# First half's scores ahead of the second half's transposes, the k loads in one run, tile 0's v on SyncE's queue, ScalarE's tables first

## The chip, the cores and the metric

The kernel runs on one core of one Trainium2 chip. A core has five engines that work beside each other: TensorE (PE, matrix products), VectorE (DVE), ScalarE (ACT), GpSimd (POOL) and SyncE (SP, which here only issues transfers). Each engine works through its own list of instructions in order. Transfers between the chip's main memory (HBM) and the on-chip memory are issued by an engine and carried out by 16 DMA engines that all queues share. In this kernel GpSimd's transfers show up in the profile as queue q0 ("software_dynamic"), SyncE's as q1 ("hardware_dynamic"), ScalarE's one transfer as q10.

The metric is the device time of one execution in microseconds. Three runs of the kernel before took 316.43, 315.59 and 316.18 us: a median of 316.18.

## The reference

Retention (attention with a decay in place of the softmax) over 8 batches, 8 heads, 576 positions, 64 numbers per head, followed by a two-layer network with a gated nonlinearity:

```
B, H, S, D_ = 8, 8, 576, 64
scores = (1/sqrt(D_)) * q @ k.T
gamma  = 1 - 2 ** (-5 - head)
Dmat   = where(i >= j, gamma ** (i - j), 0)
x      = (scores * Dmat) @ v            # -> [B * S, H * D_] = [4608, 512]
h      = x @ w_in                       # [4608, 2048]
g      = h * tanh(log(1 + exp(h)))
out    = g @ w_out                      # [4608, 512]
```

Inputs and output are float32; the kernel multiplies in bfloat16.

## The kernel before

The 4,608 rows of x are cut into 36 chunks of 128 rows, and four chunks make a tile of 512 rows. The first two tiles are special: they hold the first chunk (positions 0 to 127) of each of the 8 batches, where nothing comes from earlier positions, so that x is only masked scores times v. Tile 0 is batches 0 to 3. This text is about how tile 0 gets started; from tile 1 on the kernel is unchanged.

For tile 0 the work goes in these steps, each in two halves of two batches (g = 0 is batches 0 and 1, g = 1 is batches 2 and 3):

1. Loads. q of batch b (256 KB, float32) is issued by SyncE, line 120. k of batch b is issued by GpSimd and turned into bfloat16 on the way (`load_first_qk`, line 106). v comes in pairs of batches, 512 KB each, from GpSimd (`load_first_v`, line 117). The first layer's weights w_in come in four loads of 512 columns (512 KB each in bfloat16, from twice as many bytes in HBM), also from GpSimd (`load_w_in`, line 86). q and k are read in runs of 2 KB (eight positions of one head), v in runs of 256 B (one position of one head).
2. q is cast to bfloat16 by one instruction per batch, on different engines (lines 442, 448, 145).
3. `f_transpose(0, g, i, parts)` turns k (i = 1) or q (i = 0) of two batches on TensorE, 32 small products into PSUM, and copies the result out in two parts, on ScalarE or VectorE (line 202).
4. `f_scores(0, g)` makes 16 products (line 211) and VectorE multiplies each batch by the decay mask (line 215, one instruction per batch, `sm`).
5. `f_v(0, b, engine)` casts v of a batch (line 222). `f_out(0, b, engine)` multiplies masked scores by v (line 236) and copies into x transposed (line 239).
6. `g1(0, f, half)` is the first layer for 128 of the 2,048 columns. For f = 0 to 3 it is done on the first two batches' rows (`half[0]`, line 466) and later on the others (`half[1]`, line 470). From f = 4 on all 512 rows go together (line 497). ScalarE applies the nonlinearity (Mish, line 373).

`keep_warm(n)` issues n products of zeros on TensorE, to keep it busy in stretches where it would wait. ScalarE loads a table before its first exponential and another before its first Mish; a one-number Mish (`warm`, line 457) brings the second load on early. The decay mask is made from `dist` by 8 VectorE instructions (line 153) and one exponential (line 440); `gq` and `gv`, used from tile 1 on and in `f_state`, are exponentials of `ex` (lines 447, 455, 456), which comes from `pos`.

The order of all this is written out by hand: each engine does its instructions in the order of the program, and waits only on data and on buffers. So the order in which GpSimd meets its loads, its casts (`pool` in the calls) and its small set-up instructions is the order of the source, from line 121 on and then from line 440 on. Behind GpSimd's casts of v in the source stand the loads of tile 1's k and q (line 472), the second layer's weights w_out (line 474) and further loads.

q, k and v of tile 0 lie in two buffers that later hold the results of the first layer: `stage` (k, q in bfloat16 and v) and `gts[0]` (q in float32).

Of the kernel before, what the change touches and what calls it, by code (L numbers as in the profile page):

```python
# [10 lines left out]
F32 = mybir.dt.float32  # L11
BF16 = mybir.dt.bfloat16
# [5 lines left out]
def kernel(  # L18
# [18 lines left out]
    nc = tc.nc  # L37
    B, H, S, D = q.shape
    assert (B, H, S, D) == (8, 8, 576, 64)
    P = 128  # L40
# [21 lines left out]
    consts = ctx.enter_context(tc.tile_pool(name="consts", bufs=1))  # L62
    wpool = ctx.enter_context(tc.tile_pool(name="weights", bufs=1))
    first = ctx.enter_context(tc.tile_pool(name="first", bufs=1))
# [7 lines left out]
    ps_sc = ctx.enter_context(tc.tile_pool(name="ps_sc", bufs=2, space=PS))  # L72
    ps_st = ctx.enter_context(tc.tile_pool(name="ps_st", bufs=1, space=PS))
    ps_h = ctx.enter_context(tc.tile_pool(name="ps_h", bufs=2, space=PS))
    ps_o = ctx.enter_context(tc.tile_pool(name="ps_o", bufs=1, space=PS))
# [9 lines left out]
    def load_w_in(f0, n):  # L85
        nc.gpsimd.dma_start(out=w_in_t[:, :, ds(f0, n)], in_=w_in_r[:, :, ds(f0, n)])
# [8 lines left out]
    stage = gp.tile([P, nF, NCH * P], BF16, name="gT")  # L95
    gts = {0: gp.tile([P, nF, NCH * P], BF16, name="gT")}
    q0 = gts[0][:, H:nF, :].bitcast(F32).rearrange("p (b a) c -> p b (a c)", a=2)
    v0 = {}
    fst = {}

    def load_first_qk(t, i, b):

        name = ("qb", "kb")[i]
        if t not in fst:
            fst[t] = {"qb": stage[:, 0:4, :], "kb": stage[:, 4:8, :], "vb": {}}
        nc.gpsimd.dma_start(out=fst[t][name][:, b, :],  # L106
                            in_=(q, k)[i][4 * t + b, :, 0:P, :].rearrange("h (g r) d -> g h (r d)", r=8))

    def load_first_v(b):

        if b < 4:
            pair = stage[:, ds(8 + 2 * b, 4), :].bitcast(F32).rearrange("p a (c d) -> p (a c) d", d=D)
        else:
            pair = first.tile([P, 2 * H, D], F32, name="vpair", bufs=2)
        for e in range(2):
            v0[b + e] = pair[:, ds(H * e, H), :]
        nc.gpsimd.dma_start(out=pair, in_=v[ds(b, 2), :, 0:P, :].rearrange("b h p d -> p (b h) d"))

    for b in range(4):
        nc.sync.dma_start(out=q0[:, b, :], in_=q[b, :, 0:P, :].rearrange("h (g r) d -> g h (r d)", r=8))  # L120
    for b in range(2):
        load_first_qk(0, 1, b)

    zeros = consts.tile([P, 512], BF16)
    nc.vector.memset(zeros, 0.0)
# [4 lines left out]
                   allow_small_or_imprecise_dtypes=True)  # L130
    nc.gpsimd.affine_select(out=dist, in_=dist, compare_op=OP.is_ge, fill=1.0e6,
                            base=0, pattern=[[1, P]], channel_multiplier=-1)
    ident = consts.tile([P, P], BF16)
    make_identity(nc, ident)
    for b in (2, 3):
        load_first_qk(0, 1, b)
    pos = consts.tile([P, 5], F32)
    nc.gpsimd.iota(pos, pattern=[[P, 5]], base=0, channel_multiplier=1,
                   allow_small_or_imprecise_dtypes=True)
    nc.gpsimd.iota(pos[64:P, 4:5], pattern=[[1, 1]], base=512, channel_multiplier=1,  # L140
                   allow_small_or_imprecise_dtypes=True)
    load_first_v(0)
    load_w_in(0, 512)
    load_first_v(2)
    nc.gpsimd.tensor_copy(fst[0]["qb"][:, 3, :], q0[:, 3, :])
    for i in range(1, 4):
        load_w_in(512 * i, 512)
    mask = consts.tile([P, P], F32)
    mask2 = consts.tile([P, P], F32)
    lg = [math.log(1.0 - 2.0 ** (-5.0 - h)) for h in range(H)]  # L150
# [13 lines left out]
    def keep_warm(n, pool=ps_o, name="ops"):  # L164
        idle = pool.tile([P, 512], F32, name=name)
        for _ in range(n):
            nc.tensor.matmul(idle, lhsT=zeros[:, 0:P], rhs=zeros, start=True, stop=True)
# [14 lines left out]
    def f_transpose(t, g, i, parts):  # L182

        name = ("qb", "kb")[i]
        out_t = first.tile([P, H, P], BF16, name=name + "T", bufs=2)
        n = 8 // len(parts)
        moves = []
        for j, (pool, tname, copy) in enumerate(parts):
            tp = pool.tile([P, 2, 8, P] if tname == "sc" else [P, 8, P], BF16, name=tname)
            tp = (tp[:, 0] if tname == "sc" else tp)[:, 0:n]  # L190
            for r in range(n):
                if t == 1:
                    mix = fst[1][name, "mix", g][:, n * j + r]
                    nc.tensor.transpose(tp[:, r, :], mix.rearrange("p x d -> p (x d)"), ident)
                else:
                    for x in range(2):
                        nc.tensor.transpose(tp[ds(64 * x, 64), r, :],
                                            fst[0][name][:, 2 * g + x, ts(n * j + r, D)], ident)
            moves.append((copy, out_t.rearrange("p h (g r) -> p h g r", r=8)[:, :, :, ds(n * j, n)],
                          tp.rearrange("p r (g h) -> p h g r", h=H)))  # L200
        for copy, to, src in moves:
            copy(to, src)
        fst[t][name, g] = out_t

    def f_scores(t, g, between=None):
        qT, kT = fst[t]["qb", g], fst[t]["kb", g]
        scs = [ps_sc.tile([P, 2, NP, P], F32, name="sc").rearrange("p a b i -> p (a b) i") for _ in range(2)]
        for h in range(H):
            for x in range(2):
                r = ds(64 * x, 64)  # L210
                nc.tensor.matmul(scs[x][:, h, :], lhsT=kT[r, h, :], rhs=qT[r, h, :], start=True, stop=True)  # L211
        for x in range(2):
            b = 2 * g + x
            sm = first.tile([P, H, P], BF16, name="sm0", bufs=4)
            nc.vector.tensor_tensor(sm, scs[x], dmask, op=OP.mult)  # L215
            fst[t]["sm", b] = sm
            if between and x == 0:
                between()

    def f_v(t, b, copy):  # L220
        vb = first.tile([P, H, D], BF16, name="vb", bufs=4)
        copy(vb, v0[4 * t + b])
        fst[t]["vb"][b] = vb

    def f_out(t, b, copy):
        if b == 0:
            xts[t] = xp.tile([P, KC, NCH * P], BF16, name="xT")
        vb = fst[t]["vb"][b]
        if t == 0:
            pool, name = ((ps_h, "hp"), (ps_h, "hp"), (ps_st, "st"), (ps_o, "ops"))[b]  # L230
            ot = pool.tile([P, NP, P], F32, name=name)
        else:
            ot = ps_sc.tile([P, 2, NP, P], F32, name="sc")[:, 0]
        for p in range(NP):
            for e in range(2):
                nc.tensor.matmul(ot[ds(64 * e, 64), p, :], lhsT=vb[:, 2 * p + e, :],
                                 rhs=fst[t]["sm", b][:, 2 * p + e, :],
                                 start=(p == 0), stop=True, skip_group_check=True)
        copy(xts[t][:, :, ts(b, P)], ot)  # L239
# [196 lines left out]
    dve, act, pool = nc.vector.tensor_copy, nc.scalar.copy, nc.gpsimd.tensor_copy  # L436
# [1 line left out]

    half = (slice(0, 2 * P), slice(2 * P, 4 * P))
    nc.scalar.activation(dmask, dmask, AX.Exp, bias=lnd[:, 0:1])  # L440
    for b in range(2):
        dve(fst[0]["qb"][:, b, :], q0[:, b, :])
    keep_warm(8)
    f_transpose(0, 0, 1, [(ps_h, "hp", act), (ps_h, "hp", dve)])
    f_transpose(0, 0, 0, [(ps_st, "st", act), (ps_o, "ops", dve)])
    for h in range(H):
        nc.vector.tensor_scalar(ex[:, :, h], pos, lg[h], None, op0=OP.mult)
    act(fst[0]["qb"][:, 2, :], q0[:, 2, :])
    f_transpose(0, 1, 1, [(ps_h, "hp", act), (ps_h, "hp", act)])
    keep_warm(2, ps_sc, "sc")  # L450
    f_scores(0, 0)
    keep_warm(3, ps_st, "st")
    f_transpose(0, 1, 0, [(ps_st, "st", act), (ps_o, "ops", act)])
    keep_warm(4, ps_h, "hp")
    nc.scalar.activation(gq, ex, AX.Exp)
    nc.scalar.activation(gv, ex, AX.Exp, scale=-1.0)
    nc.scalar.activation(warm, lnd, AX.Mish)
    f_v(0, 0, pool)
    f_v(0, 1, pool)
    f_scores(0, 1, lambda: f_out(0, 0, dve))  # L460
    f_out(0, 1, act)
    f_v(0, 2, pool)
    f_v(0, 3, act)
    keep_warm(3, ps_st, "st")
    for f in range(4):
        g1(0, f, half[0])
    f_out(0, 2, act)
# [14 lines left out]
    for b in (4, 6):  # L482
        load_first_v(b)
# [147 lines left out]
```

## Time and profile before

| what | value |
|---|---|
| time of three runs | 316.43, 315.59, 316.18 us, median 316.18 |
| the profiled execution | 317.75 us, of which the span from first to last instruction is 316.0 |
| TensorE (PE) busy | 302.7 us, 96% of the span |
| VectorE, ScalarE, GpSimd busy | 135.3, 111.7, 143.0 us |
| TensorE's mean granted clock | 0.989 of full speed |
| moved by the DMA engines | 42.85 MB, 136 GB/s on average |
| q0 (GpSimd), q1 (SyncE) | 27.27 MB in 48,640 packets; 15.08 MB in 24,832 packets |

How to read the rows. In a timeline a row gives the start, the time taken, the engine, the line of the program (L197 is line 197), the operation, output <- inputs, the shape and how many such instructions are merged; in square brackets stands how long the engine had been idle before, and what ended the wait. A row of stages gives the stretch, its length, busy time and count for each engine, the clock that TensorE was granted, the share of time in which the DMA engines were busy (it can be above 1, since packets overlap) and GB/s. A row of a queue gives packets, megabytes and the packets' time as a share of 16 engines. All times are microseconds from the start of the span. In the tables of the trace `gT` stands for the two buffers in which q, k and v of tile 0 are put.

### The profile page before, as it was taken

The numbers are of one execution on the slowest core, as the hardware profiler recorded it, in microseconds if no ns is written. First come the engines' busy times: TensorE is split into PE (matmuls) and PEld (weight loads), VectorE is DVE, ScalarE is ACT, GpSimd is POOL, SyncE is SP. The second block draws the span as 40 slices with busy tenths as digits, with TensorE's granted clock in tenths as the row PEclk, the third lists the DMA queues.
The fourth block names the chain that finished last, engine by engine and source line by source line (L and its number), as shares of the span: only waits on it lengthen the run. The fifth ranks groups of instructions, "written<-read, shape, count | busy, mean of one in ns | idle before, by whom it ended". The sixth has DMA issues, their size and how long they took to land.

```text
span 316.0 us, 5807 instructions
## 1 busy us (share of the span) xinstructions
PE 302.7 (96%) x2428; PEld 153.4 (49%) x2468; DVE 135.3 (43%) x198; ACT 111.7 (35%) x185; POOL 143.0 (45%) x178
## 2 busy tenths in 40 slices
PE   5779999999999999998999999999999999999995
PEld 2454554555555554544545454545454545444444
DVE  3553148487636535353535453535354332001111
ACT  3476525753353533332232333332323232333300
POOL 8587849889684976356373536252010000000000
PEclk9599999999999999999999999999999999999999
DMA  7999999999992899999999999991514000010031
GB/s 176 232 207 204 221 207 197 274 163 183 234 183 79 139 163 164 187 83 210 153 181 88 214 136 180 122 168 36 98 37 100 35 33 35 34 33 33 35 97 69
DMA packets 73642, 42.85 MB, mean 136 GB/s; under 512 B 58640, under 2 KB 64528, under 8 KB 73616
## 3 DMA queue, kind: packets, MB, share of 16 engines
q0 software_dynamic: 48640, 27.27, 64.0%
q1 hardware_dynamic: 24832, 15.08, 25.9%
q8 instruction: 19, 0.31, 0.5%
q10 hardware_dynamic: 144, 0.13, 0.1%
q14 instruction: 7, 0.06, 0.1%
HBM read 38.80 MB, written 9.44 MB: 153 GB/s over the span
## 4 chain that ended last, share of the span: by engine, by line
PE 74%; DMA 20%; POOL 3%; issue 1%; ACT 0%; DVE 0%; POOLq 0%
PE hp L371 31%; PE ops L386 26%; DMA qkT<-qks 9%; PE hp L386 4%; DMA w_out_t<-in_moe_w_out_dram 4%; DMA qraw<-in_q_dram 4%; PE sc L301 2%; DMA vraw<-in_v_dram 2%; PE st L333 2%; DMA gT<-in_k_dram 2%; PE sc L353 1%; PE sc L358 1%; PE sc L288 1%; PE hp L414 1%; POOL gT L106 1%
## 5 line engine op out<-in xcount | busy, mean ns | idle before, releaser
L371 PE MATMUL hp<-xT,w_in_t 128*128 128x512 bf16 (+1 forms) x562 | 141.4, 373 | 2.9 <-DVE xT L239 0.8
L373 ACT ACTIVATE gT<-hp 128x512 bf16<-128x512 f32 (+1 forms) x148 | 86.8, 586 | 157.7 <-PE hp L371 143.9
L386 PE MATMUL ops<-w_out_t,gT 128*128 128x512 bf16 x430 | 110.1, 379 | 0.4
L371 PEld LDWEIGHTS <-w_in_t 128*128 128x128 bf16 x592 | 55.1, 98 | 62.8 <-issue 2.1
L386 PEld LDWEIGHTS <-gT 128*128 128x128 bf16 x496 | 48.3, 98 | 58.0 <-issue 0.8
L422 DVE COPY res<-ops 128x512 f32<-128x512 f32 x28 | 19.3, 688 | 83.4 <-PE ops L386 79.6
L336 DVE TENSOR_TENSOR ssb<-st,diag 128x512 bf16<-128x512 f32 x32 | 21.9, 685 | 49.6 <-PE st L333 49.6
L263 POOL DMA_DIRECT2D qraw<-in_q_dram x24 | 22.1, 921 | 40.5 <-DVE qks L273 38.0
L279 POOL TENSOR_TENSOR vs<-vraw,gv 128x512 bf16<-128x512 f32 x28 | 29.9, 1077 | 20.2 <-issue 14.0
L305 DVE TENSOR_TENSOR sm<-sc,mask 128x1024 bf16<-128x1024 f32 x28 | 33.1, 1216 | 5.9 <-PE sc L301 5.9
L263 POOL DMA_DIRECT2D vraw<-in_v_dram x24 | 21.7, 903 | 2.6 <-DMA vpair<-in_v_dram 1.5
L263 POOL DMA_DIRECT2D qks<-in_k_dram x24 | 21.6, 899 | 1.2 <-DMA w_out_t<-in_moe_w_out_dram 0.9
L273 DVE TENSOR_TENSOR qks<-qraw,gq 128x512 bf16<-128x512 f32 x28 | 19.9, 746 | 0.0
L362 DVE CAST xT<-sc 128x512 bf16<-128x512 f32 x24 | 15.3, 680 | 0.0
L386 PE MATMUL hp<-w_out_t,gT 128*128 128x512 bf16 x61 | 14.7, 379 | 0.2
L215 DVE TENSOR_TENSOR sm<-sc,dmask 128x1024 bf16<-128x1024 f32 x8 | 9.5, 1220 | 8.4 <-PE sc L211 8.4
L289 ACT COPY qkT<-sc 128x1024 bf16<-128x1024 bf16 x10 | 10.1, 1010 | 8.0 <-PE sc L288 8.0
L267 POOL DMA_DIRECT2D qraw<-in_q_dram x8 | 5.6, 708 | 14.1 <-DVE qks L273 14.1
L301 PE MATMUL sc<-qkT 64*128 64x128 bf16 x224 | 9.4, 218 | 1.5 <-DMA qkT<-qks 1.5
L301 PEld LDWEIGHTS <-qkT 64*128 64x128 bf16 x224 | 6.3, 94 | 6.7 <-issue 3.4
L353 PE MATMUL sc<-qkT,ssb 128*64 128x128 bf16 (+1 forms) x224 | 9.5, 213 | 0.0
L358 PE MATMUL sc<-sm,vs 128*64 128x128 bf16 x192 | 9.4, 219 | 0.0
(102 smaller groups left out, 193.3 us busy)
## 6 DMA issues: line engine op xcount, KB each, us to landing
out_dram<-res SPq DMA_DIRECT2D x31, 256.0 KB, 3.9
qraw<-in_q_dram POOLq DMA_DIRECT2D x24, 256.0 KB, 5.5
vraw<-in_v_dram POOLq DMA_DIRECT2D x24, 256.0 KB, 8.3
qks<-in_k_dram POOLq DMA_DIRECT2D x24, 128.0 KB, 7.3
w_in_t<-in_moe_w_in_dram POOLq DMA_DIRECT2D x4, 512.0 KB, 10.6
w_out_t<-in_moe_w_out_dram POOLq DMA_DIRECT2D x4, 512.0 KB, 10.4
gT<-in_q_dram SPq DMA_DIRECT2D x4, 256.0 KB, 4.9
gT<-in_k_dram POOLq DMA_DIRECT2D x8, 128.0 KB, 6.9
```

What stands on the lines that cost most here:

```text
L263: nc.gpsimd.dma_start(out=t, in_=src[b, :, ds(P * c, P), :].rearrange("h p d -> p h d"))
L273: nc.vector.tensor_tensor(live[n]["qks"][:, 0], live[n]["q"], gq[:, c, :].unsqueeze(2).to_broadcast([P, H, D]), op=OP.mult)
L279: nc.gpsimd.tensor_tensor(vs, live[n]["v"], gv[:, c, :].unsqueeze(2).to_broadcast([P, H, D]), op=OP.mult)
L301: nc.tensor.matmul(sc[:, e, p, :], lhsT=qk[r, 1, p, :], rhs=qk[r, 0, p, :], start=True, stop=True)
L305: nc.vector.tensor_tensor(sm.rearrange("p e n i -> p (e n) i"), sc.rearrange("p e n i -> p (e n) i"), m.unsqueeze(1).to_broadcast([P, 2 * ...
L336: nc.vector.tensor_tensor(ssb.rearrange("p e n d -> p e (n d)"), st.rearrange("p n d -> p (n d)").unsqueeze(1).to_broadcast([P, 2, NP * 64 ...
L353: nc.tensor.matmul(ot[ds(64 * e, 64), p, ds(i0, iw)], lhsT=st_sb[bb, cc][:, e, p, :], rhs=qk[:, 0, p, ds(i0, iw)], start=(i0 == 0 and p == ...
L362: nc.vector.tensor_copy(xts[t][:, :, ts(s, P)], ot)
L371: nc.tensor.matmul(hp[:, cols], lhsT=w_in_t[:, c, ts(f, P)], rhs=xts[t][:, c, cols], start=(c == 0), stop=(c == KC - 1))
L373: nc.scalar.activation(gts[t][:, f, cols], hp[:, cols], AX.Mish)
L386: nc.tensor.matmul(ops, lhsT=gts[t][:, f, ts(s, P)], rhs=w_out_t[:, f, :], start=(f == 0), stop=(f == nF - 1))
L422: copy(ot, ops)
```

## The change

In the loads:

- tile 0's v goes from two loads of two batches on GpSimd to four loads of one batch on SyncE, behind the four loads of q;
- the four k loads stand together on GpSimd, behind the two instructions that make `dist`, and ahead of `pos` and the identity; before, two stood at the very start and two after the identity;
- three of the four w_in loads then follow at once, ahead of the cast of batch 3's q; the fourth follows the cast.

In the order written out by hand:

- `ex`, `gq`, `gv` and the first Mish, with its table load, move ahead of the transposes;
- `f_scores(0, 0)` moves ahead of the second half's transposes of k; the second half's transposes of q follow directly on those of k;
- the cast of batch 2's q goes from ScalarE to VectorE, the cast of batch 3's v from ScalarE to GpSimd, so that all four v casts stand together on GpSimd;
- `f_out(0, 0)` and `f_out(0, 1)` stand ahead of `f_scores(0, 1)`; before, `f_out(0, 0)` stood between its two masks and `f_out(0, 1)` after it;
- the numbers of warming products are 9, 2, 3 and 4 in place of 8, 2, 3, 4 and 3.

```
     def load_first_v(b):
-        if b < 4:
-            pair = stage[:, ds(8 + 2 * b, 4), :].bitcast(F32).rearrange("p a (c d) -> p (a c) d", d=D)
-        else:
-            pair = first.tile([P, 2 * H, D], F32, name="vpair", bufs=2)
+        pair = first.tile([P, 2 * H, D], F32, name="vpair", bufs=2)
...
     for b in range(4):
         nc.sync.dma_start(out=q0[:, b, :], in_=q[b, :, 0:P, :].rearrange("h (g r) d -> g h (r d)", r=8))
-    for b in range(2):
-        load_first_qk(0, 1, b)
+    for b in range(4):
+        v0[b] = stage[:, ds(8 + 2 * b, 2), :].bitcast(F32).rearrange("p a (c d) -> p (a c) d", d=D)
+        nc.sync.dma_start(out=v0[b], in_=v[b, :, 0:P, :].rearrange("h p d -> p h d"))
...
     nc.gpsimd.affine_select(out=dist, in_=dist, compare_op=OP.is_ge, fill=1.0e6,
                             base=0, pattern=[[1, P]], channel_multiplier=-1)
-    ident = consts.tile([P, P], BF16)
-    make_identity(nc, ident)
-    for b in (2, 3):
+    for b in range(4):
         load_first_qk(0, 1, b)
     pos = consts.tile([P, 5], F32)
...
-    load_first_v(0)
-    load_w_in(0, 512)
-    load_first_v(2)
+    ident = consts.tile([P, P], BF16)
+    make_identity(nc, ident)
+    for i in range(3):
+        load_w_in(512 * i, 512)
+
     nc.gpsimd.tensor_copy(fst[0]["qb"][:, 3, :], q0[:, 3, :])
-    for i in range(1, 4):
-        load_w_in(512 * i, 512)
+    load_w_in(1536, 512)
...
     nc.scalar.activation(dmask, dmask, AX.Exp, bias=lnd[:, 0:1])
-    for b in range(2):
-        dve(fst[0]["qb"][:, b, :], q0[:, b, :])
-    keep_warm(8)
-    f_transpose(0, 0, 1, [(ps_h, "hp", act), (ps_h, "hp", dve)])
-    f_transpose(0, 0, 0, [(ps_st, "st", act), (ps_o, "ops", dve)])
     for h in range(H):
         nc.vector.tensor_scalar(ex[:, :, h], pos, lg[h], None, op0=OP.mult)
-    act(fst[0]["qb"][:, 2, :], q0[:, 2, :])
-    f_transpose(0, 1, 1, [(ps_h, "hp", act), (ps_h, "hp", act)])
-    keep_warm(2, ps_sc, "sc")
-    f_scores(0, 0)
-    keep_warm(3, ps_st, "st")
-    f_transpose(0, 1, 0, [(ps_st, "st", act), (ps_o, "ops", act)])
-    keep_warm(4, ps_h, "hp")
     nc.scalar.activation(gq, ex, AX.Exp)
     nc.scalar.activation(gv, ex, AX.Exp, scale=-1.0)
     nc.scalar.activation(warm, lnd, AX.Mish)
-    f_v(0, 0, pool)
-    f_v(0, 1, pool)
-    f_scores(0, 1, lambda: f_out(0, 0, dve))
+    for b in range(2):
+        dve(fst[0]["qb"][:, b, :], q0[:, b, :])
+    keep_warm(9)
+    f_transpose(0, 0, 1, [(ps_h, "hp", act), (ps_h, "hp", dve)])
+    f_transpose(0, 0, 0, [(ps_st, "st", act), (ps_o, "ops", dve)])
+    dve(fst[0]["qb"][:, 2, :], q0[:, 2, :])
+    keep_warm(2, ps_sc, "sc")
+    f_scores(0, 0)
+    f_transpose(0, 1, 1, [(ps_h, "hp", act), (ps_h, "hp", act)])
+    f_transpose(0, 1, 0, [(ps_st, "st", act), (ps_o, "ops", act)])
+    for b in range(4):
+        f_v(0, b, pool)
+    keep_warm(3, ps_h, "hp")
+    f_out(0, 0, dve)
     f_out(0, 1, act)
-    f_v(0, 2, pool)
-    f_v(0, 3, act)
-    keep_warm(3, ps_st, "st")
+    f_scores(0, 1)
+    keep_warm(4, ps_st, "st")
     for f in range(4):
         g1(0, f, half[0])
     f_out(0, 2, act)
```

## The prediction

> **What bounds the kernel now.** I read the page's head, then busy time by stages, then TensorE's timeline of the first 24 us, the waits there, and last the packets of each DMA queue in short windows. The stages come first, since an average over the whole says nothing about a change in the first 22 us:
>
> ```profile
> span 316.0 us, 5807 instructions
> ...
> 8.55:12.00 3.45, 2.16 (x22) 1.28 (x25) 1.54 (x10) 1.75 (x4) 2.85 (x5) 0.50 1.12 230
> ...
> 18.90:22.40 3.50, 2.63 (x32) 1.96 (x32) 1.77 (x3) 2.09 (x5) 3.48 (x5) 1.00 1.24 206
> 22.40:110.00 87.60, 86.73 (x787) 46.39 (x803) 48.56 (x63) 42.97 (x68) 68.71 (x83) 1.00 1.19 190
> ```
>
> (Columns: stretch, length, busy PE, weight loads, DVE, ACT, POOL, granted clock, DMA share, GB/s.) From 22.40 to 110 PE is busy 86.73 of 87.60 us. So the end is set by when the second half-pass of the first layer starts (line 470, 22.41), and what moves that start moves the end by about as much. The DMA share is over 1 from 3.5 us on: transfers, too, are short in this stretch. TensorE before that start:
>
> ```profile
> 7.19 0.63 PE L197 MATMUL hp<-ident,gT 128*64 128x128 bf16 x15 [1.94 <-DMA gT<-in_k_dram]
> ...
> 9.82 1.06 PE L197 MATMUL hp<-ident,gT 128*64 128x128 bf16 x15 [0.41 <-DMA gT<-in_k_dram]
> ...
> 11.78 1.13 PE L211 MATMUL sc<-qbT,kbT 64*128 64x128 bf16 x16
> ...
> 18.95 2.10 PE L371 MATMUL hp<-xT,w_in_t 128*128 128x256 bf16 x16 [0.68 <-ACT vb L222]
> ...
> 22.41 1.79 PE L371 MATMUL hp<-xT,w_in_t 128*128 128x256 bf16 x13 [0.79 <-DVE xT L239]
> ...
> POOL vb L222 <- DMA gT<-in_v_dram: 3.7, 2, 3.3
> ```
>
> The reader sees the order: k0 and k1 land at 7.19, k3 at 9.82, scores at 11.78 and (a row left out) 16.33. The last line, from the waits, says that GpSimd's casts waited 3.7 us for v, and nobody waited for them. The packets decide the rest:
>
> ```profile
> DMA packets 73, 0.30 MB, mean 239 GB/s; under 512 B 0, under 2 KB 0, under 8 KB 73
> ...
> DMA packets 409, 0.41 MB, mean 206 GB/s; under 512 B 7, under 2 KB 409, under 8 KB 409
> ...
> q1 hardware_dynamic: 98, 0.18, 106.6%
> ...
> q1 hardware_dynamic: 595, 0.14, 111.5%
> q0 software_dynamic: 618, 0.14, 85.3%
> ```
>
> Line 1 (9.25 to 10.5) is v from GpSimd's queue: 4 KB packets made out of 256 B runs of HBM. Line 2 (11 to 13) is w_in there: 1 KB packets, 204 a microsecond, or 78 ns on each of 16 engines. Line 3 (6.25 to 7) is q on SyncE's queue: 1.9 KB a packet, one 2 KB run each; that queue shows no packet longer than a run. The last pair (136 to 140) has both queues in backlog: equal packets from both, whatever they hold (505 and 513 in another stretch, 153.5 to 156).
>
> **The change part by part.** The profiled execution took 317.75 us for a span of 316.0, 1.57 us above the median of the runs, 316.18. I work out the shift of the start at 22.41 and add it to the median.
>
> *GpSimd's order.* The k's come behind iota and select (0.30 + 0.29), without identity and the gap between pairs. Issues at 1.32, 2.02, 3.79, 4.30 become some 1.75, 2.4, 2.95, 3.5: k0 and k1 0.4 later, k2 and k3 0.8 earlier. The engines are saturated, so the last of q and k still ends near 8.5; k1's landing, 7.15, moves by -0.2 to +0.4: I take +0.2. Identity is ready at 5.1 instead of 3.85, before the transposes. The w_in issues (0.77 each) come from 6.36 to 5.2; they queue behind the k's all the same.
>
> *Tables and casts.* ex (1.03 on DVE) goes from 9.07 to 4.6, and q0's cast from 4.87 to 5.6: under the wait for k1. gq, gv, table load and first Mish (0.25 + 0.24 + 1.28 + 0.20) go from 15.99 to about 5.7, ending at 7.8, where ACT's first copy was due at 7.64: at worst 0.2 late. q2's cast moves from ACT to DVE (0.5). One more warming matmul (0.43) lies under the same wait.
>
> *Scores first.* The first pair's transposes are copied out by 9.15 (DVE 8.47 + 0.68). The warming pair runs meanwhile, so scores(0,0) go from 11.78 to 9.4, at half clock until 10.5. Masks are two by 1.22 to 13.0. k2, k3 transposes follow at 10.5, q2, q3 by 12.5; copies end at 13.4, three warming matmuls at 13.8. If v is there, f_out(0,0), f_out(0,1) take 0.9, scores(0,1) 1.06 to 15.8, masks to 18.2, first half-pass 16.7 to 18.5, f_out(0,2), f_out(0,3) and their copies 1.4. The second half-pass starts at 19.9: 2.5 us earlier. This is the gain.
>
> *v on SyncE's queue.* GpSimd saves 1.21 + 1.17 of issue, which nothing waited for. SyncE issues four more at 3.4 and on; its next issue is at 50.63, so a blocked queue there (two transposes, of 256 B packets, took it 4.56 at 110) costs nothing. What matters is when v lands, and the trace has no load of 256 B runs on this queue. Bounds: 2 KB packets as q's or better, or 256 B packets. I take 256 B: on this queue q's 2 KB run, ACT's 1 KB half rows (144 packets, 0.13 MB) and the transposes' 256 B all went as one packet per run. Then v0 starts at 8.5 against w_in, packet for packet. A 256 B packet took 20 to 29 ns an engine (820 a microsecond at 141.2, 544 at 148); beside w_in's 78 a pair takes 98 to 107 ns, so each queue gets 150 to 163 a microsecond. w_in's four loads hold 2,112 packets with their completions; v0 and v1 hold 2,080. So v0 ends at 15.1 and v1 only as w_in does: 8.5 + 13.2 = 21.7, landed 1.0 later (k3's last packet 8.75, landed 9.77) at 22.7. v2, v3 follow alone (696 a microsecond from 148 to 149: 3.0 us), landing by 25.7.
>
> *The new wait.* f_out(0,1) stands ahead of scores(0,1) on PE, and GpSimd's casts (0.62 each) stand ahead of everything it issues next: the second tile's k and q (before: 16.99), w_out (19.05), the state products. From 22.7: cast 0.62, f_out 0.9, scores 1.06, four warming matmuls 1.7, first half-pass 1.8 to 3.4, last f_outs 0.65, copy 0.8: 7.5 to 9.1 at half clock, some 6.7 if the clock comes back one step sooner. With 7.2: 29.9, or 7.5 us late. The half clock is this trace's: 0.50 from 8.55 to 15.4, after 3.45 us with 1.23 busy; PE would now idle from 17.5 to 22.7.
>
> The loads behind GpSimd lose less: the DMA queue reached the second tile's k at 22.8 and would at about 27.3, 4.5 later against a PE 7.5 later; k, q were read at 27.35, w_out at 35.85 (landed 29.9). No second wait.
>
> *Two rules.* The Trainium skill's page DMA: Bandwidth & Descriptors (Queues, rings and completion order; Issuing engines are not separate DMA queues) says that an engine switches queues at packets, and that another issuing engine saves issue time only. The equal counts above agree; the rule speaks against this move, and by it alone v gains no bandwidth and the sum is scores-first, -2.5; packet sizes make it +7.5. TensorE: Matmul & The Clock Gate (Part 1) gives an idle window of 3.4 us as the price of half clock; this trace halved it with a longest gap of 1.94 us. By the rule the first scores would run at full clock (0.5 less); the trace decides.
>
> **The rivals.** *A, v arrives in time: faster.* If the hardware queue joins runs to 2 KB packets, a pair takes 136 ns (16 engines over 118 a microsecond, from 0.24 MB a microsecond) + 78 = 214, a v takes 1.7 us: landings 11.2, 12.9, 14.6, 16.3, all ahead of their use. Then -2.5 holds, from -3.2 (v no matter, k early) to -1 (half clock until the half-pass): 313.0 to 315.2, middle 313.7. For it speak 4 KB packets of the same v on GpSimd's queue; against it, every row of SyncE's. The point of decision is v1's landing: at 15.2, with 7.2 behind it, comes the old start; v3 must land by 19.9.
>
> *B, v only partly starved.* If w_in's issues leave gaps (GpSimd's issue waited 2.0 for w_in at 25.27) or v is served two for one, v1 lands at 15 to 18: -0.2 to +2.8, 316 to 319.
>
> *C, nothing shows.* The masks on DVE (4 by 1.22) and the copies still order the chain, and k1 comes 0.4 later: the gain shrinks under 0.9 us: 315.3 to 317.1.
>
> **How the numbers follow.** Likeliest: starvation, +7.5 on 316.18 = 323.7, chance 0.62, its own range 322.5 to 326 (v1 landed at 22.3 with 6.7 behind it, to 23.4 with 9.1). A 0.27; B 0.07; C 0.04. One kernel's runs spread by 0.27% here, so 0.3%, 0.95 us, is about what tells from no change. Faster: A but for its weakest and a little of B, 0.27; same 0.05; slower 0.68. Leaving A out would leave over 2 in 10, so the range runs from 313.3, within A, to 326: the sum of what is left outside is some 0.14.
>
> **What would show it.** Right: SyncE's queue moves some 1,040 packets per v, counts equal to GpSimd's between 9 and 21 us, POOL's wait on v from 3.7 to over 10 us, PE idle ahead of line 236, clock 0.50 past 22 us, half-pass two near 30. Scores at 9.4 and ACT's table load under 8 us show the other parts. Wrong: v at 2 KB a packet with landings by 17; or v1 served ahead of w_in, then the second half-pass near 20 and the clock back by 15.4. A k1 later than 7.6 would make the reorder worth less than put here.

## The result, and the profile after

The changed kernel took 325.38 us (median of four runs, 325.14 to 328.02), the kernel before 316.0 on the same occasion: a ratio of 1.0316, 95% interval 1.026 to 1.0371. It is slower by 9.4 us. Here and below, medians are over all runs, while ratios are estimated without the few runs in which the chip was in its slower state (one of four of the last experiment, one of twelve of before beside the pair on the order of k), so that a ratio need not be the quotient of the medians. The profiled execution of after took 325.58 us with a span of 323.9 and a mean clock of 0.984.

From the page of after: the span; the DMA queues with their packets, megabytes and share of the engines; the chain by engine; and the group of `f_out`'s products (line 233 here, 236 in before; all lines of after shown below are three lower than before's, and those of the experiments are shifted in the same way).

```profile
span 323.9 us, 5854 instructions
...
q0 software_dynamic: 48352, 26.22, 59.0%
q1 hardware_dynamic: 28992, 16.13, 26.1%
...
PE 91%; DMA 6%; SPq 1%; DVE 0%; POOL 0%; issue 0%
...
L233 PE MATMUL hp<-sm,vb 128*64 128x128 bf16 x16 | 1.1, 270 | 9.0 <-POOL vb L219 9.0
```

SyncE's queue has 4,160 packets more than before (24,832), which is four loads of 1,040, and 1.05 MB more, which is all of v. 256 KB in runs of 256 B makes 1,024 of each load's 1,040. On GpSimd's queue the same v had taken 288 packets (48,640 before). The 6% of DMA in the chain are the wait for this v (before's chain held 20% of DMA, for other loads and for transposes); TensorE lost 9.0 us in front of 16 small products.

TensorE's and GpSimd's timeline of after says where:

```profile
8.52 1.06 PE L194 MATMUL hp<-ident,gT 128*64 128x128 bf16 x15 [2.16 <-DMA gT<-in_k_dram]
...
11.34 1.13 PE L208 MATMUL sc<-qbT,kbT 64*128 64x128 bf16 x16
...
16.61 0.61 POOL L219 CAST vb<-gT 128x512 bf16<-128x512 f32 x1 [5.17 <-DMA gT<-in_v_dram]
...
17.28 0.41 PE L233 MATMUL hp<-sm,vb 128*64 128x128 bf16 x8 [2.77 <-POOL vb L219]
...
23.29 0.61 POOL L219 CAST vb<-gT 128x512 bf16<-128x512 f32 x1 [6.07 <-DMA gT<-in_v_dram]
...
23.96 0.64 PE L233 MATMUL hp<-sm,vb 128*64 128x128 bf16 x8 [6.26 <-POOL vb L219]
24.53 1.03 PE L208 MATMUL sc<-qbT,kbT 64*128 64x128 bf16 x16
25.50 1.89 PE L164 MATMUL st<-zeros 128*128 128x512 bf16 x4
27.18 3.27 PE L368 MATMUL hp<-xT,w_in_t 128*128 128x256 bf16 x16
...
31.80 4.47 PE L368 MATMUL hp<-xT,w_in_t 128*128 128x256 bf16 x26 [0.79 <-DVE xT L236]
```

v0 could be cast at 16.61 and v1 at 23.29, each after a wait of 5 to 6 us. TensorE, with `f_out` at the head of its list, waited 2.77 and 6.26 us for these two casts. Behind v1 the work runs slowly, and the second half-pass starts at 31.80 in place of 22.41.

The packets of the two queues of after in 15 to 19 (first two lines) and in 23.5 to 24.5 (last line), and the stages (length, busy PE, weight loads, DVE, ACT, POOL, clock, DMA share, GB/s):

```profile
q0 software_dynamic: 633, 0.63, 92.9%
q1 hardware_dynamic: 607, 0.15, 28.9%
...
q1 hardware_dynamic: 806, 0.20, 92.5%
...
18.90:22.40 3.50, 0.00 (x0) 0.00 (x0) 0.00 (x0) 0.00 (x0) 0.00 (x0) 0.61 1.21 197
22.40:25.80 3.40, 1.84 (x25) 1.30 (x26) 0.20 (x1) 0.59 (x1) 1.17 (x2) 0.50 0.82 158
...
32.60:110.00 77.40, 77.33 (x680) 40.32 (x678) 43.97 (x54) 38.09 (x61) 59.54 (x71) 1.00 1.19 189
```

In 4 us each queue got some 620 packets, but w_in 0.63 MB for them and v 0.15 MB: an equal share of the packets gave v a fifth of the bytes. With w_in gone, v's queue alone did 806 packets a microsecond. While v trickled in, no engine but GpSimd, for one cast, did anything from 18.90 to 23.96, and TensorE's clock fell to half (0.50 in the next stage). From 32.6 to 110 nothing more is lost (77.33 of 77.40).

### The profile page after: what moved, and what is told of

Read it like the earlier page. It is cut to its first block, busy times and chain, and to the rows that moved or that the text cites. A ratio compares the mean times of both kernels' runs of the same rounds, so it can differ in the third digit from the quotient of the medians.

```text
span 323.9 us, 5854 instructions
## 1 busy us (share of the span) xinstructions
PE 306.3 (95%) x2466; PEld 154.8 (48%) x2466; DVE 136.8 (42%) x199; ACT 110.8 (34%) x183; POOL 142.0 (44%) x177
## 3 DMA queue, kind: packets, MB, share of 16 engines
q0 software_dynamic: 48352, 26.22, 59.0%
## 4 chain that ended last, share of the span: by engine, by line
PE 91%; DMA 6%; SPq 1%; DVE 0%; POOL 0%; issue 0%
PE hp L368 40%; PE ops L383 29%; DMA gT<-in_v_dram 6%; PE hp L383 4%; PE sc L298 2%; PE st L330 2%; PE hp L400 2%; PE sc L350 2%; PE sc L355 2%; PE sc L285 1%; PE st L400 1%; PE ops L400 1%; PE hp L411 1%; SPq L117 1%; PE sc L208 1%; PE st L164 1%
## 5 line engine op out<-in xcount | busy, mean ns | idle before, releaser
L368 PE MATMUL hp<-xT,w_in_t 128*128 128x512 bf16 (+1 forms) x592 | 145.3, 377 | 0.9 <-DVE xT L236 0.8
L368 PEld LDWEIGHTS <-w_in_t 128*128 128x128 bf16 x592 | 56.0, 99 | 62.6 <-DVE xT L236 1.3
L359 DVE CAST xT<-sc 128x512 bf16<-128x512 f32 x24 | 15.4, 682 | 0.0
L233 PE MATMUL hp<-sm,vb 128*64 128x128 bf16 x16 | 1.1, 270 | 9.0 <-POOL vb L219 9.0
```

Of the source, the lines that this page charges most:

```text
L368: nc.tensor.matmul(hp[:, cols], lhsT=w_in_t[:, c, ts(f, P)], rhs=xts[t][:, c, cols], start=(c == 0), stop=(c == KC - 1))
```

## The experiments

The theory: v starves on SyncE's queue, because its packets are 256 B long and are served one for one with w_in's 1 KB packets. Rivals: the queue or its issuing as such is slow; w_in in front is all that matters; the clock, or the place of `f_out` ahead of the scores, makes most of the loss. The medians of one experiment are set against those of before on the same chip (315.84 for the first four, 315.73 for the pair on the order of k, 315.47 for the other four). For orientation: in all profiled executions but three the span ends 291.7 to 292.1 us after the second half-pass starts, so the start tells the time. The three are before (293.6) and two experiments, whose extra losses are shown where they come.

**v back on GpSimd, and w_in's loads back in their place among v's and behind the cast of batch 3's q; all else as in after.**

```
-    for b in range(4):
-        v0[b] = stage[:, ds(8 + 2 * b, 2), :].bitcast(F32).rearrange(...)
-        nc.sync.dma_start(out=v0[b], in_=v[b, :, 0:P, :].rearrange("h p d -> p h d"))
...
-    for i in range(3):
-        load_w_in(512 * i, 512)
+    load_first_v(0)
+    load_w_in(0, 512)
+    load_first_v(2)
     nc.gpsimd.tensor_copy(fst[0]["qb"][:, 3, :], q0[:, 3, :])
-    load_w_in(1536, 512)
+    for i in range(1, 4):
+        load_w_in(512 * i, 512)
```

> The changed kernel with tile 0's v back on GpSimd's queue in its two loads of 512 KB, where they stood before; all else as changed. Theory (v on SyncE's queue is starved packet for packet by w_in, and that alone costs): v0 and v1 land near 12, v2 and v3 near 16.5, nobody waits for them, and the scores-first order shows its gain: second half-pass near 20, 313.0 to 315.0 us. Rival 1 (the order is the cause: v's products ahead of the second scores on TensorE, four casts in a row on GpSimd): still 320 or more. Rival 2 (k's new order, with k1 landing at 8.5 instead of 7.2, eats the gain): 315.3 to 317.

Measured: 314.32 us (ten runs), ratio 0.9952 (0.9928 to 0.9975). TensorE's timeline of this kernel, the transposes of k1 and the second half-pass:

```profile
8.62 1.03 PE L195 MATMUL hp<-ident,gT 128*64 128x128 bf16 x15 [2.38 <-DMA gT<-in_k_dram]
...
21.25 12.67 PE L369 MATMUL hp<-xT,w_in_t 128*128 128x256 bf16 x64 [0.79 <-DVE xT L237]
```

The whole loss is gone with v's move undone, and the rest of the change is a small gain. (w_in's place, which went back with v's, is tried by itself further down and changes nothing there.) k1's transposes still start at 8.62, against 7.19 before: that part of the change came out differently from the forecast and is taken up below.

**Only v moved, all else as before.** The four SyncE loads are added to before, its two `load_first_v` of tile 0 left out.

> The kernel before with one part of the change: tile 0's v in four loads on SyncE's queue behind q; order of everything else as before. Theory: v1 lands at 22 to 23 as in the changed kernel; the second scores and their masks are done by then, so behind v1 stand only cast, product, copy, first half-pass at half clock, v2 and v3: second half-pass at 28 to 30, 321.5 to 323.5 us. Rival 1 (the order is the cause): within 1 us of before, 315 to 317.

Measured: 327.15 us (four runs), ratio 1.037 (1.0325 to 1.0415), more than any theory had. The waits of the first 34 us, TensorE's second part of the first half-pass, and two stages:

```profile
ACT vb L220 <- DMA gT<-in_v_dram: 6.2, 1, 6.2
...
PE hp L369 <- ACT gT L371: 5.7, 1, 5.7
...
26.61 1.87 PE L369 MATMUL hp<-xT,w_in_t 128*128 128x256 bf16 x8 [5.66 <-ACT gT L371]
...
30.26:34.00 3.74, 3.74 (x17) 2.48 (x18) 2.11 (x3) 1.26 (x4) 3.74 (x5) 0.50 1.21 198
34.00:38.00 4.00, 4.00 (x16) 1.66 (x15) 0.00 (x0) 2.06 (x4) 3.71 (x8) 0.81 1.24 201
```

The move alone costs 11.3 us (327.15 against 315.84), by another door. v1 is here in time (cast at 14.72, since w_in's last three loads are issued only at 9.71). v3 is not: its cast stands on ScalarE ahead of the nonlinearity, waits 6.2 us, and TensorE waits 5.7 for ScalarE. The second half-pass starts at 30.26, earlier than in after, yet the span is longer: it begins at half clock, and (1 - 0.50) x 3.74 + (1 - 0.81) x 4.00 = 2.6 us are lost there.

**v on the same queue, in 2 KB runs.** The same bytes are read in q's pattern, eight positions of a head at a time. Tile 0 then gets v's rows in another order, so it computes something else at the same cost.

```
-        nc.sync.dma_start(out=v0[b], in_=v[b, :, 0:P, :].rearrange("h p d -> p h d"))
+        nc.sync.dma_start(out=stage[:, ds(8 + 2 * b, 2), :].bitcast(F32).rearrange("p a c -> p (a c)"),
+                          in_=v[b, :, 0:P, :].rearrange("h (g r) d -> g h (r d)", r=8))
```

> The changed kernel with v of tile 0 read in q's pattern: the same 256 KB a batch on the same queue in the same place, but in runs of 2 KB in place of 256 B, so that tile 0 gets v's rows in another order (its output is then another). Theory (packet length): 144 packets a batch in place of 1,040; v0 lands near 12.5, v3 by 18, second half-pass at 20 to 21.5, 313.5 to 315.5 us. Rival 3 (what is queued behind q on SyncE is late whatever its runs): v as late as in the changed kernel, 322 to 326.

Measured: 313.95 us (nine runs), ratio 0.9943 (0.9922 to 0.9964). The queues in 9 to 15, and the second half-pass:

```profile
q1 hardware_dynamic: 550, 0.99, 59.2%
q0 software_dynamic: 589, 0.57, 56.6%
...
20.03 12.67 PE L369 MATMUL hp<-xT,w_in_t 128*128 128x256 bf16 x64 [0.79 <-DVE xT L237]
```

This is the run that decides. Queue, place, bytes and all of w_in in front are those of after; only the run length differs, and the 11 us are gone. The packet counts are again nearly equal (550 and 589), but SyncE's queue now gets 0.99 MB to 0.57. In after the same 6 us read:

```profile
q0 software_dynamic: 834, 0.82, 81.6%
q1 hardware_dynamic: 1453, 0.38, 38.0%
```

There v got more packets than w_in, since w_in's queue had little to send at first (201 packets to 844 of v from 9 to 11); from 11 to 23 the two are equal (1,882 and 1,846). Even so, 1,453 packets of v held only 0.38 MB. With the long runs the casts of v start at 12.13 to 16.37, and TensorE waits for none of them.

**TensorE kept busy through the wait for v.**

```
-    keep_warm(3, ps_h, "hp")
+    keep_warm(16, ps_h, "hp")
     f_out(0, 0, dve)
+    keep_warm(28, ps_st, "st")
     f_out(0, 1, act)
```

> The changed kernel with TensorE kept busy through the wait for v: 16 warming products in place of 3 ahead of f_out(0,0), and 28 new ones between f_out(0,0) and f_out(0,1); nothing else. Theory (part of the loss is the half clock after the wait): first half-pass 1.8 instead of 3.3 us, scores 0.6 instead of 1.06, warming four 0.9 instead of 1.9: second half-pass near 29 instead of 31.8, 322 to 323.2 us. Rival 4 (the clock plays no part): 325 to 326. v's landings should not move.

Measured: 323.01 us (four runs), ratio 1.023 (1.0196 to 1.0264). The stage that was empty in after, and the half-passes:

```profile
18.90:22.40 3.50, 3.50 (x18) 1.60 (x17) 0.00 (x0) 0.00 (x0) 0.00 (x0) 1.00 1.22 196
...
25.32 2.11 PE L368 MATMUL hp<-xT,w_in_t 128*128 128x256 bf16 x16
...
28.79 5.55 PE L368 MATMUL hp<-xT,w_in_t 128*128 128x256 bf16 x31 [0.79 <-DVE xT L236]
```

The clock stays at 1.00 and the first half-pass takes 2.11 in place of 3.27. Of the loss of 9.4 us the clock is some 2.4 (325.38 - 323.01, medians of two occasions). The rest is not: 323.01 - 315.84 = 7.2 us are left with the clock at 1.00.

**w_in's last three loads behind v's casts.**

```
-    for i in range(3):
-        load_w_in(512 * i, 512)
+    load_w_in(0, 512)
     nc.gpsimd.tensor_copy(fst[0]["qb"][:, 3, :], q0[:, 3, :])
-    load_w_in(1536, 512)
...
     for b in range(4):
         f_v(0, b, pool)
+    for i in range(1, 4):
+        load_w_in(512 * i, 512)
```

> The changed kernel with three of the four w_in loads issued behind GpSimd's four casts of v; v stays on SyncE's queue in its 256 B packets. Theory (it is w_in's backlog, packet for packet, that starves v): w_in0 is through near 13.5, then v has the engines alone at some 800 packets a microsecond (the changed kernel's rate from 23.5 to 24.5); v1 lands near 16, v3 by 18.5 to 19.5, second half-pass near 22; w_in1 is issued at about 20 and may come late by up to 3 us: 315.5 to 319 us. Rival 3' (256 B packets on this queue are slow by themselves, at 155 a microsecond whatever else runs): v1 at 23, 324 us or more.

Measured: 317.4 us (ten runs), ratio 1.0063 (1.0043 to 1.0084). SyncE's queue in 13 to 17, the second half-pass, and two stages:

```profile
q1 hardware_dynamic: 3091, 0.78, 92.8%
...
22.05 12.24 PE L365 MATMUL hp<-xT,w_in_t 128*128 128x256 bf16 x62 [0.79 <-DVE xT L233]
...
18.90:22.40 3.50, 2.67 (x35) 1.96 (x33) 2.37 (x4) 2.08 (x5) 3.50 (x6) 1.00 0.57 77
32.60:110.00 77.40, 76.25 (x730) 40.55 (x728) 47.82 (x60) 36.22 (x56) 64.11 (x77) 1.00 1.30 201
```

With w_in out of the way v goes at 773 packets a microsecond, and all four casts start between 15.07 and 18.26. So it needs both: short packets and a rival with long ones. Alone, the 256 B packets carry 0.20 MB a microsecond, against 0.24 for q's 2 KB packets in the forecast's rows (0.18 MB in 0.75 us). Still, v1's cast starts at 16.14 in place of 13.22 with long runs, and the second half-pass 2.0 us later (22.05 to 20.03); k1's transposes start 0.56 later in this execution, which is part of it. And the delay has a price later: the DMA engines are half idle (0.57) until 22.4, and TensorE then loses 1.15 us up to 110, 0.30 of it waiting for a load of w_out and 0.85 for a copy on ScalarE (why that copy is late was not tried). Holding the rival back gets most of the loss back (317.4 against 325.38) but stays 3.5 us above the long runs (313.95).

**The old order of the k loads as well.** On top of the kernel with v back, k0 and k1 are issued at the very start and k2, k3 behind the identity, as in before.

```
+    for b in range(2):
+        load_first_qk(0, 1, b)
...
-    for b in range(4):
+    ident = consts.tile([P, P], BF16)
+    make_identity(nc, ident)
+    for b in (2, 3):
         load_first_qk(0, 1, b)
...
-    ident = consts.tile([P, P], BF16)
-    make_identity(nc, ident)
```

> The kernel with v back on GpSimd and, further, k and the identity in the order of before: k0 and k1 at the very start, k2 and k3 behind the identity. What is left of the change is scores first, tables first and the casts. Theory (k's new order costs 1.3 us in k1's landing, 8.6 against 7.2): first transposes near 7.2, and the start of the second half-pass 0.5 to 1.3 earlier than with v back alone (21.25): 312.8 to 313.8 us against 314.3. Rival (k1 is not what the chain waits for, GpSimd's casts are: v0 at 14.8 there): 313.9 to 314.8.

Measured: 312.87 us (twelve runs), ratio 0.9931 (0.9909 to 0.9953), second half-pass at 18.95. Since this interval overlaps that of the kernel with v back, and the two ran on different chips, the pair was run once more on one chip:

> v on GpSimd as before, the k loads and identity in the order of after: the kernel of the run with v put back, run again beside the one that has the old order, on one chip. Theory (the new order of the k loads costs, since k1 lands some 1.3 us later): 314.0 to 314.8 us, and 0.8 to 2.0 us above the kernel with the old order. Rival (the 1.5 us between those two came from two chips and from whether TensorE was at half clock in the one profiled execution): less than 0.5 us above it, both between 312.7 and 314.0.

> v on GpSimd and the k loads and identity in the order of before, only the handwritten order of the rest as in after. Theory (the new order of the k loads costs): 312.5 to 313.3 us, 0.8 to 2.0 us under its partner with the new order, k1's transposes some 1.3 us earlier. Rival (chips and the clock): within 0.5 us of its partner.

Measured, six runs each: 313.87 us with the new order of k (ratio 0.994, 0.9916 to 0.9963) and 312.53 with the old one (0.9902, 0.988 to 0.9925). k1's transposes and the second half-pass, first with the new order:

```profile
8.31 1.06 PE L195 MATMUL hp<-ident,gT 128*64 128x128 bf16 x15 [1.88 <-DMA gT<-in_k_dram]
...
20.04 2.12 PE L369 MATMUL hp<-xT,w_in_t 128*128 128x256 bf16 x16 [0.79 <-DVE xT L237]
```

and with the old one:

```profile
7.36 1.06 PE L198 MATMUL hp<-ident,gT 128*64 128x128 bf16 x15 [1.83 <-DMA gT<-in_k_dram]
...
18.89 3.39 PE L372 MATMUL hp<-xT,w_in_t 128*128 128x256 bf16 x20 [0.79 <-DVE xT L240]
```

The six times of each do not overlap (313.53 to 314.11; 312.36 to 313.42). The new order of the k loads costs 1.3 us: k1 lands 0.95 later, and the second half-pass starts 1.15 later. One execution says little about the start, though: the kernel with the new order started it at 21.25 when it was first run (v back on GpSimd) and at 20.04 here. It is the medians and the two sets of times that show the cost. The kernel with the old order, that is, the change without its moves of loads (v, k and w_in), is the best so far: 0.7% under before in the first of its two runs, 1.0% in the second.

**Two of w_in's loads ahead of the cast of batch 3's q, on the best version.** The kernel with v and k in their old places, with `load_w_in` for the second and third part put in front of GpSimd's cast of q3, which is the order of w_in and cast that after has.

> As the one with k's order of before, and GpSimd issues w_in1 and w_in2 before it waits for batch 3's q, w_in3 after it. Theory (with v back, GpSimd reached v0's cast at 14.8 only because it waited for q3 at 12.0 and then issued three loads of 0.75): v0 cast near 12.5, f_out(0,0) at 13 to 14 instead of 15.5, second half-pass at 19.5 to 20.5: 312.3 to 313.5 us. Rival (GpSimd is not the wait): the same as without this step.

Measured: 312.91 us (ten runs), ratio 0.9933 (0.9903 to 0.9964), second half-pass at 19.18. GpSimd's first casts of v:

```profile
12.26 1.18 POOL L224 CAST vb<-gT 128x512 bf16<-128x512 f32 x2 [0.98 <-DMA gT<-in_v_dram]
```

No further gain, and no loss: without this step the cast starts at 12.09, and here GpSimd waits 0.98 us for v itself. The loads of w_in that stood ahead of the cast were not what held it up.

**The second scores ahead of `f_out` in after.**

```
+    f_scores(0, 1)
     keep_warm(3, ps_h, "hp")
     f_out(0, 0, dve)
     f_out(0, 1, act)
-    f_scores(0, 1)
-    keep_warm(4, ps_st, "st")
```

> The changed kernel with scores(0,1) ahead of f_out(0,0) and f_out(0,1) on TensorE, and without the four warming products behind them; v stays on SyncE's queue. Theory (v sets the start, the order adds what stands behind v1): scores 1.0 and warming 1.7 leave the chain behind v1's cast at 23.3 to 23.9; second half-pass near 29.3 instead of 31.8, 322.3 to 323.8 us. Rival 1 (the order is the main cause): below 319.

Measured: 325.25 us (four runs), ratio 1.0286 (1.0241 to 1.0331): no different from after within the intervals, so the gain of 2 us or so did not show. From this kernel's timeline, v1's cast and the half-passes:

```profile
24.27 0.62 POOL L219 CAST vb<-gT 128x512 bf16<-128x512 f32 x1 [6.06 <-DMA gT<-in_v_dram]
...
26.25 3.57 PE L368 MATMUL hp<-xT,w_in_t 128*128 128x256 bf16 x16 [0.68 <-ACT xT L236]
...
31.44 2.74 PE L368 MATMUL hp<-xT,w_in_t 128*128 128x256 bf16 x18 [0.79 <-DVE xT L236]
```

Behind v1's cast 31.44 - 24.27 = 7.17 us remain, in place of 8.51 in after: 1.34 saved of the 2.7 expected, with the first half-pass still at half clock (3.57). In this one execution v1 came 0.98 later than in after, and k1 0.94 later (9.46 against 8.52), and most of the saving went there. Why it came later was not tried. The place of `f_out` is at most a small part of the loss.

## Why the prediction was right, and where its terms were off

The likeliest case, starvation, is what happened: 325.4 against 323.7 forecast, within its own range of 322.5 to 326. The mechanism is shown: run length alone takes the loss away. How near v1's arrival came is in part luck, as said below. Each step:

- *Run length and packets.* Right. One packet per 256 B run; nearly equal counts of 152 and 158 a microsecond (607 and 633 in 4 us) where 150 to 163 were forecast. The run with 2 KB runs shows that the packet's size is the cause, and not the queue. (Of the three rows that the forecast took for this, ScalarE's half rows went on queue q10 and not on SyncE's; q and the transposes stand.) The Trainium skill's page DMA: Bandwidth & Descriptors (Queues, rings and completion order) has the engine switch queues at packets, which fits these counts; its section Issuing engines are not separate DMA queues, that another issuing engine saves only issue time, understates it here: the move did not merely gain nothing, alone it cost 11.3 us (1.037).
- *v's arrival.* v1 was forecast to land at 22.7; its cast started at 23.29. v2 and v3 by 25.7; cast at 25.24 and 26.22. So 0.6 of the 1.9 us by which the start of the second half-pass (29.9 forecast, 31.80 measured) was missed. The picture behind it was too even: it let v0 and then v1 advance alike on all 16 engines from 8.5 on. In the trace each load ends in 16 landings; v0's are spread from 10.39 to 16.56, nine of them before 11.2, and v1's from 13.65 to 23.24. The casts wait for the last (16.61 and 23.29). So v as a whole had a head start, which does not show in the time because the slowest part of each load kept to the forecast's pace; that the last landings came so near it is in part luck, and why some parts are that slow was not tried.
- *Behind v1.* The mis-sized term. It was given 7.5 to 9.1 at half clock, some 6.7 if the clock came back sooner, and 7.2 was taken; it took 31.80 - 23.29 = 8.5. The clock was at half until about 29.9 (mean of 0.56 in 29.5 to 30), through nearly all of the first half-pass (3.27). With 8.5 in place of 7.2 the sum would have been 325.0. The run that kept TensorE busy needed 28.79 - 22.88 = 5.9, so half clock is 2.6 of the 8.5.
- *GpSimd's order.* Wrong in size. k1's landing was put at +0.2, within -0.2 to +0.4. It was 1.3 later in after (8.52 to 7.19) and 0.95 in the pair on one chip, worth 1.3 us in time. The reasoning was that saturated engines end q and k at the same time whatever the order, so that k1 moves little. That did not hold: the last of the k loads, which had landed at 9.77 before, landed at 10.83 in after, though it was issued earlier (7.6 us from issue to landing in place of 5.5). In the pair, k1 was issued some 0.2 us later with the new order and took 6.1 us in place of 5.3; the two k loads issued behind it took a median of 7.4, and q's last 7.5, against 5.1 and 5.9. That k1's packets share the engines with more of the others would explain it; no run shows that by itself.
- *Scores first.* Forecast -2.5, a size that was too small. With the new order of k the second half-pass started at 20.04 and, with long runs, 20.03 in place of 22.41, but at 21.25 in the first run with v back; in time the two runs with v back are 314.32 - 315.84 = -1.5 and 313.87 - 315.73 = -1.9. k1's lateness is in these. With the old order of k it is -3.5 at the start (18.89) and -3.2 in time. So a reorder that was worth more and a k1 that came later partly cancelled. In the execution with the old order the first scores start at 10.18 (forecast 9.4), the second at 13.83, where the forecast had about 14.8. Half speed early on hardly matters there: in that execution the transposes at 7.36 ran slowly (1.06 us for 15), in the other one of the same kernel not (0.63 at 7.29), and the second half-pass started at 18.89 and 18.95. Which part of the reorder gives the gain, and how much of it is the longer stretch at half clock that before has (0.50 from 8.55 to 15.4), was not tried.
- *Tables and casts.* Right: the table load and the first Mish of ScalarE were over at 6.9 (forecast 7.8), ahead of its first copy at 9.20.
- *No second wait.* Right: 77.33 of 77.40 us busy from 32.6 to 110. The DMA engines did run partly empty while GpSimd's casts held its loads (share 0.38 in 25.8 to 29.2), but TensorE came to wait for none of them.
- *The second half-pass sets the end.* Right for after: its start moved by 9.4 and the median by 9.4. The profiled spans differ by 7.9 only, since before's profiled execution lost 1.5 us more later on: TensorE waited that long for transposes by DMA (`qkT`), which it did not in after's.

The rivals: A, v in time, had the right time for its condition: 313.7 forecast, 313.95 (0.9943) with 2 KB runs. Its condition, that this queue joins runs, does not hold. For B (partly starved) w_in would have had to leave gaps; it left one, from 9 to 11, but none from 11 to 23, and v1 came at 23.3 and not at 15 to 18. For C the masks and copies would have had to order the chain; the wait on v did.

The Trainium skill's page TensorE: Matmul & The Clock Gate (Part 1) gives an idle window of 3.4 us for half clock. In after the granted clock fell at about 19.7 (mean of 0.85 in 19 to 20, 0.50 from 20 on). TensorE had then been idle for only 2.0 us, since 17.69, with 0.41 us of work since 14.51. The products say the same of an earlier place: the 15 transposes at 8.52 took 1.06 us, as at half clock before (9.82), and not 0.63 as at 7.19 there, after a longest idle stretch of 2.16 us. So here, too, it takes less than an idle stretch of 3.4 us, as in before.

## What to carry to other kernels

Before a load is moved to another queue, count its packets on that queue from its runs of HBM, and ask what else is in flight: in these runs two queues in backlog got equal packets, so a load of short runs got the smaller share of bytes, by the ratio of the packet lengths. If a load of 256 B runs must share, leave it where it goes as long packets, or read it in longer runs; holding the rival back got only part of the loss back here. A load is there when its slowest part is, so a mean rate can flatter it. And test a change of several parts apart: here the moves of v and k hid that the reorder alone is worth 0.7 to 1.0%.

## What the runs showed of the hardware that was not expected

- The granted clock can read 1.00 while TensorE is slow. In after it reads 1.00 in 9 to 18.9, yet the first scores (16 products) took 1.13 us at 11.34, and 0.62 for the same work in the run that had TensorE kept busy (at 23.90). The same holds for the run with the old order of k, which reads 1.00 in every stage from 5 to 18.9. The durations of like instructions are the better witness.
- The way back to full clock has no fixed length in these runs. With v back on GpSimd the clock came back about 3.5 us after steady work began (8.62 to about 12.1); in after it took about 6.0 (23.96 to 29.94).
- SyncE was itself held by the long list of short packets: issuing the four loads of v took it 15.6 us in after (3.46 to 19.06), while q's four loads took 2.6. Here nothing else stood on SyncE until later.
